# Filler products of a recurrent-attention and feed-forward kernel move to another PSUM bank, with a new order and engine table

## The chip, the cores and the metric

One core of one Trainium2 chip runs the whole program. The metric is the device time of one execution in microseconds (us). Times "from the span's start" count from the first instruction of the profiled execution.

## The reference

A delta-rule recurrence over 768 tokens (4 batches, 8 heads, head width 48) makes `y`; its rows, gathered to 3072 tokens of 384 features, go through a feed-forward layer with 2048 hidden features.

```python
for t in range(S):
    kt, vt, bt = (k_n[:, :, t], v[:, :, t], beta[:, :, t, None])
    y[:, :, t] = np.einsum('bhd,bhde->bhe', q[:, :, t], state)
    v_old = np.einsum('bhde,bhd->bhe', state, kt)
    state = state + bt[:, :, :, None] * np.einsum('bhd,bhe->bhde', kt, vt - v_old)
...
h = x @ w_in
sp = np.maximum(h, 0.0) + np.log1p(np.exp(-np.abs(h)))
g = h * erf(sp)
return (g @ w_out).astype(np.float32)
```

## The kernel before

**Attention.** The 768 tokens are cut into 12 chunks of 64. For each chunk TensorE forms Gram products (`gram_mm`), and DVE scales them (`gram_a`, `gram_p`). They go through DRAM into blocks (`to_dram`, `to_blocks`), and a triangular system of 32x32 blocks is solved row by row for two chunks at a time: `solve_row` (lines 341 to 353), 31 rows, two elementwise operations a row, on DVE for the first pair of chunks and on GpSimd (POOL) for the other five. Each row needs the one before it. The solution comes back (`put_blocks`, `from_blocks2`, or `back_t` and `back_x` for chunks 0 and 1) and is merged (`merge_*`). Then the recurrence runs over chunk and batch, 48 steps: `chain_u`, `chain_s` and `chain_y` on TensorE, with DVE and ScalarE (ACT) steps between (`chain_u2`, `chain_s2`, `chain_y2`, `chain_m`).

**Feed-forward.** Four steps of the recurrence make a group of 256 tokens; there are 12 groups. The input is split into a high and a low fp16 part (`x_hi`, `x_lo`), and so are the two weights, once, at the start (`w_load`, `w_mask`, `w_sign`, `w_bits`, `w_mx`, `w_hi`, `w_lo`). A group has 16 blocks of 128 hidden features. `ffn1` (line 683) is the first stage: nine products for one block. Two blocks share one PSUM bank and make a *unit*, 8 units to a group. On each unit ACT computes softplus (`e_sp`, line 715) and erf (`e_erf`, line 720), DVE multiplies the bank by the result (`e_mul`, line 724), and `e_split` and `e_rest` make the fp16 parts. `ffn2` (line 736) is the second stage: six products per block into two of three banks `pr`. Softplus and erf lie in different function tables of ACT, so `table` (line 161) loads a table (`ACT_TABLE_LOAD`, line 164) whenever the wanted one is not there.

**Banks.** PSUM has 8 banks: three for the attention (`psa`), two for the first stage (`ps1`, tag `ph`), three for the second (`pr[0]` to `pr[2]`). A buffer of a pool is given to a new tile when every use of the old tile is past. Group g's `ffn2` uses `pr[2g % 3]` and `pr[(2g + 1) % 3]`: group 0 uses `pr[0]` and `pr[1]`, group 1 `pr[2]` and `pr[0]`. At the start `pr` also serves Gram products, the splitting of `w_in` (`w_lo1`), and the first four recurrence steps.

**Filler products.** `warm` (line 174) multiplies a zero tile by itself into a bank that it takes once from `ps1`; nothing reads it. It runs 15 times at the start, and 264 events `fill` (line 181) issue one such product each at chosen places of TensorE's queue.

```python
    def warm(n):
        if not wp:
            wp.append(ps1.tile([P, FW], F32, tag="ph", name="warm"))
        for _ in range(n):
            te.matmul(wp[0], zero[:, :P], zero, start=True, stop=True)
    def fill():
        warm(1)
```

**Order and engines.** Every step is an event, registered by `on`. `ORDER` (line 34) is a permutation of the 2505 events, written out by hand, and the events are issued in it; each engine, and SyncE's queue (SP) of DMA issues, works through its own instructions in that order. `ENG` (line 35) names an engine for 17 events in place of the step's own choice (`pick`, line 112). Before the first `ffn1` TensorE's queue holds 15 + 182 filler products; behind it stand 82, the last two just ahead of the spread of group 2's maximum (`x_all` of group 2).

Of the kernel before, what the change touches and what calls it, by code (L numbers as in the profile page):

```python
# [15 lines left out]
P = 128  # L16
# [18 lines left out]
ENG = {374: "G", 488: "V", 758: "A", 766: "A", 783: "V", 790: "A", 820: "A", 937: "V", 1051: "V", 1158: "V", 1319: "V", 1461: "V", 1465: "G", 1469: "G", 1663: "A", 2005: "V", 2175: "V"}  # L35
LEAD = 3
MD = 4.4
CS = 1.2
WARM = 15
C2 = 12.0  # L40
C3 = 16.0
SS2 = 12.8
S1 = -2.5
SPL = 32
XT = (0, 1)
UM = 32
DZ = 64
WG = -6
WU = 264
MT = 58  # L50
M1 = 0
WL = (0.9, 0.95, 1.0, 1.05, 1.1, 1.15, 24, 24.1, 31.0, 32.5, 34.0, 35.5)
WK = (6.0, 6.7, 7.4, 8.1, 8.8, 9.5, 28, 29, 36.0, 37.5, 39.0, 40.5)
WF = (6.6, 7.3, 8.0, 8.7, 9.4, 10.1, 28.6, 29.6, 36.6, 38.1, 39.6, 41.1)
WI = (17.0, 18.0, 19.0, 20.0, 21.0, 22.0, 31, 32, 50.5, 52.1, 53.7, 55.3)
WOT = (36, 38, 40, 42, 76, 78, 62, 86, 88, 90, 72, 74)
WD = 0.4
LPE = ("in",)
RI = "HLHLHLHLHLHH"
RO = "LHLHLHLHLHHH"  # L60
LMI = [0] * 16
# [24 lines left out]
def delta_ffn_kernel(ctx, tc, kT, qT, ktok, vtok, btok, w_in, w_out, cst, out):  # L86
    nc = tc.nc
    te, ve, se, ge, sp = nc.tensor, nc.vector, nc.scalar, nc.gpsimd, nc.sync
# [10 lines left out]
    pr = [ps2.tile([P, 512], F32, name=f"pr{i}") for i in range(PB)]  # L99
# [7 lines left out]
    def on(t, fn, *a, **kw):  # L107
        ev.append((t, len(ev), lambda: fn(*a, **kw)))
# [3 lines left out]
    def pick(d):  # L112

        return ENG.get(cur[0], d)

# [17 lines left out]
    def us(x):  # L133
        return (x - T0) / SW
# [22 lines left out]
    zero = ff.tile([P, FW], F16, tag="ob", bufs=2, name="zero")  # L157
# [13 lines left out]

    wp = []
# [7 lines that stand above are left out]

    def fill():
        warm(1)

    def clear_q():
        for t in qp[0] + qp[1]:
            ge.memset(t, 0.0)

    def clear_x():
        for t in xm[0] + xm[1]:
            se.copy(t.rearrange("p (a x) c -> p a (x c)", a=4), zero[:, :256].unsqueeze(1).broadcast_to([P, 4, 256]))  # L190
        for t in zz:
            se.copy(t.rearrange("p a h d -> p a (h d)"), zero[:, :2 * DZ].unsqueeze(1).broadcast_to([P, NP, 2 * DZ]))

    def load_cst():
        sp.dma_start(mask, cst[:, P:])
        sp.dma_start(ident, cst[:, :P])
# [582 lines left out]
    def gram(t, d, c, name):  # L779

        on(t - 1.5 * d, load_kf, c, "kpg")
        on(t - 1.45 * d, load_kf, c, "qpg")
        for i in range(2):
            on(t + 0.9 * i * d, gram_mm, c, i, name)
            on(t + (0.35 + 0.9 * i) * d, gram_a, c, i)
            on(t + (0.45 + 0.9 * i) * d, gram_p, c, i)
        on(t + 2 * d, put_p, c)

    def norm_events(sg, t, d):
        for x in range(2):  # L790
# [3 lines left out]
            on(t + (0.2 + 0.2 * x) * d, norm_sum, c)  # L794
            gram(t + (0.75 + 1.8 * x) * d, d, c, "pg")
            on(t + (2.05 + 1.8 * x) * d, to_dram, c)
        on(t - 2.3 * d, load_beta, sg)
        for i in range(6):
            on(t + (0.45 + 0.1 * i) * d, norm_ops, sg, i)

    on(-100, clear_first)
    on(-99, clear_second)
    on(-98, warm, WARM)
    for i in range(WU):
        on(us(6 + 0.17 * i), fill)
    on(us(0), clear_q)
    for i, (fn, *a) in enumerate(((load_step, 0), (load_step, 1), (load_beta, 0), (load_kf, 0, "kpg"), (load_kf, 1, "kpg"),
                                  (load_cst,))):
        on(us(0.1 + 0.05 * i), fn, *a)
    on(us(6.5), clear_x)  # L810
    on(us(19), load_q, 0)
    on(us(21), load_q, 1)
    on(us(30), w_ident)
    for sg in range(2):
        t = (4, 20)[sg]
        if sg:
            for i, (fn, a) in enumerate(((load_step, 2), (load_step, 3), (load_beta, 1))):
                on(us(14 + 0.05 * i), fn, a)
# [167 lines left out]

    ev = [ev[i] for i in ORDER] if ORDER else sorted(ev, key=lambda e: e[:2])
    E = mybir.EngineType
# [47 lines left out]
```

## Time and profile before

| | |
|---|---|
| median of 3 runs | 614.65 us (612.47 to 615.39) |
| the profiled execution's own time | 614.14 us |
| its span | 612.4 us |
| busy: TensorE, ScalarE, VectorE, GpSimd | 97%, 85%, 66%, 50% of the span |
| ACT table loads | 165, 211.7 us in all |
| filler products | 279, 392 ns each as the profile draws them |

A busy share is time in which an engine had an instruction in work. Matmuls are pipelined, so the start of one to the start of the next is a better price than the duration drawn. A row ending in `<-` names what ended the engine's idle time before that instruction.

### The profile page before, as it was taken

The page shows a single profiled execution, that of the slowest core. Times are in us where ns is not written, and L with a number is a line of the kernel's source. Part 1 is how long each engine was busy: PE and PEld are TensorE (multiplying, and loading weights), DVE is VectorE, ACT ScalarE, POOL GpSimd, SP SyncE. Part 2 cuts the span into 40 slices and gives each one's busy share as a digit, 9 for nine tenths or more (in the row PEclk, how much of TensorE's full clock was granted, in tenths as well). Part 3 has the DMA queues.
Part 4 walks back from the last instruction along what each step waited for, and adds up shares of the span by engine and source line. Part 5 has one row for each costly group of instructions (what it writes and reads, how often), then busy time and mean ns, then how long its engine had stood idle before and what let it go on. Part 6 is the DMA issues. An engine that isn't in the chain of part 4 may idle for free.

```text
span 612.4 us, 25280 instructions
## 1 busy us (share of the span) xinstructions
PE 591.3 (97%) x11043; PEld 423.4 (69%) x11043; DVE 406.8 (66%) x926; ACT 518.2 (85%) x747; POOL 304.7 (50%) x484
## 2 busy tenths in 40 slices
PE   9999889999999989979999999999999999999996
PEld 3654566666676767767777777777777777777773
DVE  3689996688768878985875986668565665336231
ACT  8979979998886688669878999789979988879873
POOL 3010224898279834987467874289863132203221
PEclk9999999999999999999999999999999999999999
DMA  8999826374554367832583224553045100100021
GB/s 279 338 291 253 220 51 172 117 160 126 111 111 114 94 158 157 195 85 84 129 181 99 76 69 114 108 120 98 1 104 132 48 15 22 28 1 14 2 52 27
DMA packets 86383, 69.74 MB, mean 114 GB/s; under 512 B 64064, under 2 KB 73408, under 8 KB 86272
## 3 DMA queue, kind: packets, MB, share of 16 engines
q1 hardware_dynamic: 86272, 68.12, 43.3%
q8 instruction: 87, 1.43, 1.0%
q14 instruction: 24, 0.20, 0.1%
HBM read 48.17 MB, written 18.87 MB: 109 GB/s over the span
## 4 chain that ended last, share of the span: by engine, by line
PE 70%; DMA 9%; DVE 9%; ACT 5%; issue 3%; POOL 2%; SPq 1%; POOLq 0%; ACTq 0%; DVEq 0%
PE ph L693 27%; PE pr L745 10%; PE pr L747 9%; PE pr L746 9%; PE pc L481 2%; DMA qp<-pp 2%; PE pc L507 2%; DMA raw_in<-w_in 2%; PE warm L179 2%; PE pg L287 2%; PE pm L444 2%; PE pc L511 1%; PE pc L495 1%; DMA raw_out<-w_out 1%; DMA k<-ktok 1%
## 5 line engine op out<-in xcount | busy, mean ns | idle before, releaser
L164 ACT ACT_TABLE_LOAD x165 | 211.7, 1283 | 2.9
L693 PE MATMUL ph<-xh,w_in 128*128 128x256 f16 x1152 | 204.7, 273 | 1.9 <-DVE L L724 1.5
L693 PEld LDWEIGHTS <-w_in 128*128 128x128 f16 x1728 | 166.4, 98 | 31.8 <-issue 3.3
L693 PE MATMUL ph<-xl,w_in 128*128 128x256 f16 x576 | 157.0, 273 | 0.3 <-issue 0.3
L117 POOL TENSOR_TENSOR H<-L,H 128x512 f16<-128x512 f32 x58 | 69.2, 1201 | 145.8 <-DVE H L124 80.8
L745 PE MATMUL pr<-w_out,H 128*128 128x384 f16 x384 | 125.6, 327 | 0.0
L747 PE MATMUL pr<-w_out,H 128*128 128x384 f16 x384 | 125.2, 326 | 0.3 <-issue 0.3
L746 PE MATMUL pr<-w_out,H 128*128 128x384 f16 x384 | 125.2, 326 | 0.0
L724 DVE SCALAR_TENSOR_TENSOR L<-ph,L 128x512 f32<-128x512 f32 x96 | 65.8, 688 | 83.8 <-ACT L L720 70.3
L353 POOL TENSOR_TENSOR xb<-xb,tmptmpg 128x31 f32<-128x31 f32 (+15 forms) x154 | 89.2, 579 | 12.1
L351 POOL TENSOR_TENSOR tmptmpg<-gb,xb 128x31 f32<-128x31 f32 (+15 forms) x154 | 83.2, 540 | 22.0 <-DMA v<-vtok 6.9
L715 ACT ACTIVATE L<-ph,xct 128x512 f32<-128x512 f32 x96 | 65.6, 687 | 28.3 <-PE ph L693 26.3
L117 POOL TENSOR_TENSOR z<-v,nm 64x192 f32<-64x192 f32 x94 | 51.6, 549 | 65.7 <-DMA v<-vtok 50.4
L179 PE MATMUL warm<-zero 128*128 128x512 f16 x279 | 72.6, 392 | 1.2 <-DVE zero L170 1.2
L720 ACT ACTIVATE L<-L 128x512 f32<-128x512 f32 x96 | 59.6, 629 | 0.9
L747 PEld LDWEIGHTS <-H 128*128 128x128 f16 x384 | 37.6, 98 | 25.5 <-issue 0.7
L745 PEld LDWEIGHTS <-H 128*128 128x128 f16 x384 | 37.5, 98 | 22.2
L746 PEld LDWEIGHTS <-H 128*128 128x128 f16 x384 | 37.6, 98 | 19.9
L179 PEld LDWEIGHTS <-zero 128*128 128x128 f16 x279 | 26.1, 100 | 30.1 <-issue 6.2
L487 DVE TENSOR_TENSOR z<-pc,ga 64x192 f32<-64x192 f32 x88 | 31.3, 355 | 17.6 <-PE pc L481 13.0
L122 ACT CAST H<-L 128x512 f16<-128x512 f32 x56 | 33.7, 610 | 9.4 <-DVE L L724 9.3
L500 DVE TENSOR_TENSOR z<-pc,z 48x192 f32<-48x192 f32 x80 | 28.3, 353 | 17.1 <-PE pc L495 13.7
(157 smaller groups left out, 823.8 us busy)
## 6 DMA issues: line engine op xcount, KB each, us to landing
raw_in<-w_in SPq DMA_DIRECT2D x12, 512.0 KB, 9.2
raw_out<-w_out SPq DMA_DIRECT2D x12, 512.0 KB, 7.6
d<-A SPq DMA_DIRECT2D x22, 256.0 KB, 3.5
d<-pp SPq DMA_DIRECT2D x10, 512.0 KB, 4.5
qp<-d SPq DMA_DIRECT2D x20, 256.0 KB, 4.2
kpg<-kT SPq DMA_DIRECT2D x24, 192.0 KB, 4.7
k<-ktok SPq DMA_DIRECT2D x12, 384.0 KB, 5.6
qp<-qT SPq DMA_DIRECT2D x24, 192.0 KB, 3.7
```

The source lines that it names most:

```text
L117: {"V": ve, "G": ge}[pick(d)].tensor_tensor(*a, **kw)
L164: se.add_instruction(mybir.InstLoadActFuncSet(name=nc.get_next_instruction_name(), act_func_set_id=i, ins=[], outs=[]))
L179: te.matmul(wp[0], zero[:, :P], zero, start=True, stop=True)
L351: eng.tensor_tensor(tv, G[:, s, s + 1:].unsqueeze(1).broadcast_to([P, ncol, nr]), Xv[:, :, s:s + 1].broadcast_to([P, ncol, nr]), op=ALU.mult)
L353: eng.tensor_tensor(Xv[:, :, s + 1:], Xv[:, :, s + 1:], tv, op=ALU.add)
L693: te.matmul(ph, w[:, i, kt * P:kt * P + P], G[x][:, :, ksl], start=(m == 0), stop=(m == 8))
L715: se.activation(unit(g, u), G["ph", u], AF.Softplus, bias=0.0, scale=G["ct"])
L720: se.activation(Lu, Lu, AF.Erf, bias=0.0, scale=1.0)
L724: ve.scalar_tensor_tensor(Lu, fg[g]["ph", u], HSC, Lu, op0=ALU.mult, op1=ALU.mult)
L745: te.matmul(G["po"][a], gh[:, o, asl], wout_h[:, i, :], start=(i == 0), stop=False)
L746: te.matmul(G["po"][a], gh[:, o, asl], wout_l[:, i, :], start=False, stop=False)
L747: te.matmul(G["po"][a], gl[:, o, asl], wout_h[:, i, :], start=False, stop=(i == NFF - 1))
```

## The change

82 filler products are taken out, all that stood behind the first `ffn1` in TensorE's queue. 50 others, `fill2`, are put in behind it; they write `pr[2]` and not the tile taken from `ps1`. They stand between `chain_s` of step 2 and `merge_e` of chunk 2. The remaining 15 + 182 all stand ahead of the first `ffn1`.

`ORDER` is a new permutation of the now 2473 events. Read by name, TensorE's queue keeps its sequence but for short moves: `ffn1` of unit 6 of group 1 moves ahead of `gram_mm` of chunk 5, and between the `ffn1` of the first two units of group 0, where a Gram product, five filler products and a merge stood, the filler products are gone. On SP, `from_blocks2` of chunk 2 moves ahead of `to_dram` of chunk 4, and the loads of the first two chunks' keys move behind nine `w_load` of `w_in`. On ACT, `clear_x` moves from the first place to behind seven steps on `w_in` and two `norm_sq`.

`ENG` now has 153 entries, and some 140 events take another engine. Between the first `ffn1` and `x_all` of group 2: 13 rows of the second and third solve go from POOL to DVE (6 of solve 1, 7 of solve 2; an eighth of solve 2 follows later, while its row 21 goes back to POOL); 14 events leave ACT (five `e_split` and two `w_hi` to POOL, the other seven to DVE) and 5 come to it; three `e_rest` go from DVE to POOL and two the other way; three `put_v` go to DVE. Ahead of the first `ffn1`: eight `w_sign` and two `w_mx` go from ACT to DVE, five `back_x` the other way, two `w_hi` to POOL, and rows 0 and 24 of the first solve to POOL. In the order of events ACT has 163 table loads, 27 between the first `ffn1` and `x_all` of group 2 where there were 31.

```diff
...
-WU = 264
+WU = 182
+WV = 50
...
+    def fill2():
+        te.matmul(pr[2], zero[:, :P], zero, start=True, stop=True)
+
...
     for i in range(WU):
         on(us(6 + 0.17 * i), fill)
+    for i in range(WV):
+        on(us(6 + 0.17 * (WU + i)), fill2)
...
```

## Rows read from the trace of the kernel before

**Rows 1.** Stretches of the span, busy us (xinstructions): PE, PEld, DVE, ACT, POOL; clock, DMA

```profile
0.00:92.00 92.00, 85.55 (x1436) 48.48 (x1437) 71.15 (x193) 79.36 (x167) 14.66 (x27) 1.00 0.82 238
92.00:134.10 42.10, 40.48 (x753) 26.89 (x751) 29.83 (x62) 39.70 (x54) 30.62 (x51) 1.00 0.61 157
134.10:178.60 44.50, 43.33 (x711) 30.81 (x710) 32.20 (x58) 39.40 (x52) 28.06 (x50) 1.00 0.49 113
178.60:194.60 16.00, 15.80 (x563) 11.59 (x563) 12.26 (x29) 10.51 (x19) 14.36 (x23) 1.00 0.23 60
194.60:230.60 36.00, 33.20 (x928) 25.65 (x927) 28.44 (x74) 28.07 (x41) 22.09 (x40) 1.00 0.57 149
230.60:312.40 81.80, 78.36 (x1682) 60.68 (x1678) 63.01 (x140) 68.44 (x94) 54.07 (x89) 1.00 0.56 132
312.40:426.00 113.60, 113.60 (x2422) 86.39 (x2421) 84.03 (x187) 99.14 (x133) 78.06 (x129) 1.00 0.44 107
```

**Rows 2.** The chain that ended last, 97 to 103 us: start, duration, engine and line

```profile
97.30 0.70 DVE L L724
...
98.05 2.14 PE ph L693 x18
...
100.21 0.69 ACT L L715
...
100.91 1.28 ACT L164
...
102.21 0.64 ACT L L720
...
102.87 0.70 DVE L L724
```

**Rows 3.** Line 724 (`e_mul`) from 91 to 200 us: min/median/max ns, first and last start

```profile
L724 DVE SCALAR_TENSOR_TENSOR L<-ph,L x16: 673/691/694, 97.3 to 198.1; 128x512 f32<-128x512 f32 x16
```

**Rows 4.** The filler products (line 179) alone, 92 to 194.6 us: PE and PEld busy

```profile
92.00:194.60 102.60, 22.66 (x83) 7.27 (x82) 1.00 0.50 123
```

**Rows 5.** TensorE in order of time, 32 to 37 us: 17 filler products and the next

```profile
32.85 3.84 PE L179 MATMUL warm<-zero 128*128 128x512 f16 x17
36.53 0.38 PE L544 MATMUL spin<-ident,m_in 128*128 128x128 f32 x2
```

**Rows 6.** `chain_s` of step 2 on TensorE, `chain_s2` of steps 2 and 1 on DVE

```profile
100.97 0.57 PE L495 MATMUL pr<-z,k 64*48 64x48 f32 x32
...
103.48 1.47 DVE L500 TENSOR_TENSOR z<-pr,z 48x192 f32<-48x192 f32 x4
```

**Rows 7.** Row 21 of solve 2, the one solved on DVE, between rows on POOL

```profile
202.11 0.61 POOL L351 TENSOR_TENSOR tmptmpg<-gb,xb 128x231 f32<-128x231 f32 x1
202.80 0.63 POOL L353 TENSOR_TENSOR xb<-xb,tmptmpg 128x231 f32<-128x231 f32 x1
...
203.46 0.39 DVE L351 TENSOR_TENSOR tmptmpg<-gb,xb 128x220 f32<-128x220 f32 x1 [1.99 <-POOL xb L353]
...
204.42 0.57 POOL L351 TENSOR_TENSOR tmptmpg<-gb,xb 128x207 f32<-128x207 f32 x1 [0.99 <-DVE xb L353]
```

**Rows 8.** A small DVE operation and two operations of POOL at the same time

```profile
150.94 2.61 DVE L253 SCALAR_TENSOR_TENSOR gn<-t,ri 128x32 f32<-128x32 f32 x1
...
151.24 2.26 POOL L117 TENSOR_TENSOR H<-L,H 128x512 f16<-128x512 f32 x2
```

**Rows 9.** SP's issues around `from_blocks2` of chunk 2 (line 393)

```profile
155.34 1.08 SPq L324 DMA_DIRECT2D d<-A  x2
156.52 3.31 SPq L393 DMA_DIRECT2D xm<-d  x4
```

**Rows 10.** ACT at the start: the second half of `clear_x`, the first step on `w_in`

```profile
5.82 3.21 ACT L192 CAST z<-zero 128x512 f32<-128x512 f16 x6
...
12.29 0.67 ACT L568 ACTIVATE raw_in<-raw_in 128x512 int32<-128x512 uint16 x1 [1.78 <-DMA raw_in<-w_in]
```

More of the change, by code (lines that the diff above doesn't have):

```diff
@@ new lines @@
+ENG = {312: "G", 336: "G", 342: "G", 351: "A", 359: "A", 360: "A", 361: "A", 362: "A", 369: "V", 372: "V", 373: "V", 379: "V", 381: "V", 382: "V", 435: "V", 436: "V", 439: "V", 440: "V", 441: "V", 442: "V", 443: "V", 456: "V", 457: "V", 582: "V", 583: "V", 662: "V", 670: "V", 689: "V", 693: "V", 702: "A", 705: "A", 710: "A", 721: "A", 726: "A", 734: "A", 740: "A", 742: "A", 743: "V", 750: "A", 751: "A", 753: "A", 758: "A", 759: "V", 785: "A", 786: "V", 788: "A", 799: "V", 801: "A", 804: "A", 806: "A", 807: "V", 818: "V", 863: "V", 880: "V", 905: "A", 925: "V", 934: "V", 939: "V", 942: "V", 1019: "G", 1024: "V", 1041: "V", 1050: "V", 1084: "V", 1104: "V", 1126: "V", 1129: "V", 1152: "V", 1163: "V", 1180: "V", 1203: "V", 1260: "V", 1265: "V", 1267: "V", 1270: "V", 1285: "V", 1287: "V", 1290: "V", 1300: "V", 1302: "V", 1305: "V", 1310: "V", 1403: "G", 1406: "G", 1429: "A", 1433: "G", 1435: "G", 1437: "G", 1439: "G", 1463: "G", 1508: "G", 1509: "G", 1513: "G", 1518: "V", 1519: "G", 1534: "V", 1544: "V", 1545: "V", 1553: "V", 1555: "V", 1592: "G", 1593: "G", 1597: "G", 1607: "G", 1618: "V", 1627: "G", 1631: "V", 1677: "G", 1681: "G", 1687: "G", 1691: "G", 1697: "G", 1701: "A", 1702: "V", 1707: "G", 1715: "A", 1721: "V", 1723: "V", 1765: "A", 1766: "V", 1780: "V", 1786: "V", 1796: "V", 1799: "A", 1844: "G", 1849: "G", 1859: "G", 1864: "V", 1865: "G", 1869: "A", 1875: "G", 1879: "A", 1938: "G", 1949: "G", 1953: "G", 1973: "V", 2012: "V", 2023: "G", 2028: "V", 2037: "A", 2038: "V", 2097: "G", 2117: "G", 2121: "A", 2143: "V", 2190: "G", 2196: "V", 2200: "G", 2219: "A", 2269: "A", 2349: "G", 2468: "V", 2471: "A"}
```

3 lines of the change are left out of this document (1 added, 2 removed).

## The prediction

> **What bounds the kernel now.** I read the busy time by stretches first. From 312 us on TensorE is busy all the time, and from 194.6 to 312 nearly so [rows 1]: there the end is set by TensorE's own work, and whatever starts that work earlier ends the kernel earlier. The clock is granted in full (2.4 GHz) in every one of these stretches. What can be won therefore lies ahead of 194.6 us, and in the 2.8 + 3.4 us that TensorE idles between 194.6 and 312.4 [rows 1].
>
> Between 92 and 194.6 us TensorE looks busy too, but 83 of its products there are fillers [rows 4]. One costs (36.53 - 32.85) / 17 = 0.216 us in a run of them [rows 5], so the 82 behind the first `ffn1` are 17.7 us of 102.6 with nothing in them. Why they are needed the chain of waits shows. It goes round a loop: `e_mul` of a unit (0.70), then `ffn1` of the next (2.14), softplus (0.69), a table load (1.28), erf (0.64), `e_mul` [rows 2]. `ffn1` starts 0.05 us after `e_mul` has ended. That is what a single first-stage bank looks like, and the code has one: `warm` holds the other from the start until its last use, and a buffer passes on only when all uses are past, so the 82 late fillers hold it until 194.6 us. One turn takes 102.87 - 97.30 = 5.57 us; the 16 units in this stretch come at (198.1 - 97.3) / 15 = 6.7 us [rows 3].
>
> **The change, part by part.** The sum is made against the profiled execution's 614.14 us, 0.5 below the median of the runs.
>
> *The bank.* The last filler to the first-stage tile now stands ahead of the first `ffn1`, so both banks turn. `ffn1` of the next unit can run while ACT works on this one, and the loop loses its 2.14 us of TensorE. What a unit then needs at least is ACT's share: two table loads, softplus and erf, 2 x 1.28 + 0.69 + 0.64 = 3.9 us [rows 2], below the 6.7 us at which units come. Here a rule can be held against the row. In the loop the erf starts 0.02 us after its table load has ended [rows 2], so a load costs 1.28 us and no more. The Trainium skill (ScalarE: Activation LUTs, section What ACT_TABLE_LOAD costs) gives about 2.66 us for each change of table, a drain included; by that a unit would need 6.6 us on ACT and the second bank would give nothing. By the rows it gives room.
>
> *TensorE's sum, 92 to 194.6 us.* The work stays but for its order; I take it as unchanged. 32 fillers fewer: 32 x 0.216 = 6.9 us. Its idle time there is 1.6 + 1.2 + 0.2 = 3.0 us [rows 1], all of which could go. Against that stands a new wait. The first `fill2` writes `pr[2]`, which `chain_s2` of step 2 on DVE still reads. In the kernel before `chain_s` ends at 101.54 and the two steps of `chain_s2` at 104.95, of which step 2 takes the first half, to 104.2 [rows 6]: 2.7 us if DVE comes to it as late as now, 0.7 us if it comes at once. Queued behind on TensorE is `merge_m` of chunk 1, and for that ACT and DVE wait. I take 2.7, the row as it stands, and 1.0 us more for one later wait of the size that a handoff between POOL and DVE shows [rows 7]. Sum: -6.9 - 3.0 + 3.7 = **-6.2 us**; at best -9.9, at worst 0, if another engine takes the place of the bank.
>
> *Can the others follow?* ACT is busy 39.7 + 39.4 + 10.5 = 89.6 of 102.6 us [rows 1]. Nine steps net leave it, 0.6 to 0.7 us each by operations of the same size [rows 2], and four table loads of 1.28: about 11 us less, 79 in 96: not the bound. DVE has 29.8 + 32.2 + 12.3 = 74.3 us [rows 1]. It takes 13 rows of the solves at 0.78 us (two operations of 0.39 [rows 7]), 10.1 us, and about 2 us net of smaller steps: 86 in 96. DVE is late next. POOL gives the rows away and takes five `e_split`; its 73.0 us [rows 1] hardly change.
>
> *The solves.* On POOL a row takes 203.43 - 202.11 = 1.32 us; the row on DVE, both handoffs included, 204.42 - 203.43 = 0.99 [rows 7]. 0.33 us a row makes 2.0 us for the 6 rows of solve 1 and 2.3 for solve 2, net of row 21 that goes back. `from_blocks2` of chunk 2 now stands ahead of `to_dram` of chunk 4, whose issue it followed directly [rows 9]; the two issues of `to_dram` are 1.1 us, and the wait for `gram_a` of chunk 4 goes with them. So the attention can follow an earlier feed-forward, and I book only solve 2, against TensorE's 6.2 us of idle time up to 312.4: **-2.3 us** (0 to -6.2). `to_dram` of chunk 4 comes later by the 3.3 us of the four issues that now precede it [rows 9], inside the several us won on solve 1.
>
> *Ahead of the first `ffn1`.* ACT is busy 79.4 of 92 us [rows 1] and loses eight `w_sign` and two `w_mx`, some 7 us. But `clear_x`, which now ends at 9.03 us, ahead of the first tile of `w_in` at 12.29 [rows 10], moves to behind seven steps on `w_in`: its cover is gone, and it costs what it takes, over twice the 3.2 us of its second half. DVE has 71.2 of 92 us and takes the ten steps. The two nearly cancel: 0, from -4 (ACT's gain counts alone) to +3 (the second half of `clear_x` counts alone). The keys loaded later delay the Gram products; `fill` covers that on TensorE, and DVE's `gram_a` has `w_sign` to do before it. Price: in the +3.
>
> *Moves of engine behind 312 us* have one answer: TensorE has no idle time there, so 0 while every engine keeps ahead.
>
> Sum: 614.14 - 6.2 - 2.3 + 0 = 605.6; set against the median, **606 us**.
>
> **Rivals.** *DVE takes the bank's place.* DVE then works 86 us of the stretch. Now it idles 28 us there. If 15 of those remain, since its steps wait for TensorE and ACT in turn, the stretch takes 101.3 us, 1.3 less than now, and with nothing won later the kernel takes 613. For it: `e_mul`, which frees the bank, stands on DVE behind solve rows. Against it: part of DVE's idle time is now the wait for erf.
>
> One more thing makes DVE later. The small step `gn` took 2.61 us, over just the time that POOL had two operations of 2.26 us running [rows 8]. The Trainium skill (SBUF — State Buffer, section Who interferes with whom) says that a DVE instruction with two SBUF inputs contends with a GpSimd instruction that reads SBUF, and the second to issue blocks until the first is done. By that each `e_split` on POOL may hold a solve row on DVE for its whole length; the trace agrees, but it does not show how often they meet.
>
> *Slower: the handoffs.* A solve row on DVE waits for POOL's row before it, and DVE can do nothing else meanwhile: 1.99 us in the one case [rows 7]. If each of the 13 rows waited so, DVE would need 86 + 26 = 112 us, the stretch would take 10 us more than now, and the kernel 624. It decides from where 13 waits exceed what DVE has left, 96 - 86 = 10 us: 0.8 us a row. Against it: rows that follow one another on DVE (6 and 7, 15 and 16, 4 to 8 of solve 2) wait once.
>
> *The start gains as well.* If ACT's relief counts in full, 4 us and some of TensorE's other idle time come on top: 600.
>
> *Nothing happens.* If the bank were not released at the last first-stage filler, the loop would stay at 5.57 us a unit, the fillers would only have been cover, and the time would be 614. The code speaks against it. The same time would come if a table load held ACT for twice what its row shows, since a unit would then need as much on ACT as the loop takes now; the erf that starts 0.02 us behind its load speaks against that [rows 2], and I give it 0.01. The figure of the Trainium skill above, taken for both loads, would lead there.
>
> **How the numbers follow.** Forecast 0.60, start gains too 0.15, DVE takes over 0.12, handoffs 0.08, nothing 0.04, long table loads 0.01. About 0.5% (3.1 us) is what a measurement of this kernel can tell from no change. Faster: 0.60 + 0.15 + 0.05 of DVE's case = 0.80; same: the other 0.07, 0.04 and 0.01 = 0.12; slower 0.08. The range reaches from the second case with some of the -9.9 bound, 598, to DVE's case, 613.
>
> **What would show it.** Right: `ffn1` of a unit no longer starts at the end of the unit's `e_mul` before it; the units of the first two groups come at under 6.4 us; 50 fillers between 92 and 190 us; `x_all` of group 2 some 6 us earlier; the first `fill2` waits for `chain_s2` on DVE. Wrong: the first `ffn1` far from 92 us; DVE busy over 95% of the stretch with `e_mul` late after erf; `e_mul` waiting on solve rows of POOL; or idle time of TensorE behind 312 us.

## The result, and the profile after

The changed kernel takes **621.09 us** (median of 4 runs, 618.95 to 624.35), against 614.25 of the kernel before beside it: a ratio of 1.0119, 95% interval 1.0074 to 1.0163. Run again, it gave 1.0153 [1.0079, 1.0227]. It is slower by over 1%, where 606 was forecast. The profiled execution took 620.85 us with a span of 619.1, 6.7 longer than before.

The stretches of the changed kernel, with the columns of [rows 1]:

```profile
0.00:92.00 92.00, 84.56 (x1365) 47.85 (x1366) 70.60 (x183) 71.00 (x150) 18.64 (x32) 0.98 0.82 240
92.00:134.10 42.10, 36.09 (x785) 25.96 (x783) 30.61 (x77) 32.48 (x45) 26.00 (x37) 0.96 0.56 135
134.10:178.60 44.50, 44.50 (x732) 32.14 (x734) 38.03 (x82) 40.00 (x55) 29.69 (x47) 1.00 0.57 127
178.60:194.60 16.00, 15.26 (x559) 11.19 (x549) 14.29 (x34) 8.97 (x18) 13.06 (x20) 1.00 0.41 92
194.60:230.60 36.00, 32.28 (x847) 25.04 (x842) 28.38 (x71) 27.66 (x39) 22.03 (x38) 0.95 0.46 120
230.60:312.40 81.80, 80.08 (x1774) 61.20 (x1766) 62.04 (x138) 69.58 (x96) 54.62 (x94) 1.00 0.62 150
312.40:426.00 113.60, 111.06 (x2367) 83.93 (x2366) 77.58 (x181) 97.83 (x129) 72.85 (x120) 1.00 0.40 97
```

Two things are new. TensorE idles where it did not, 6.0 us between 92 and 134.1 (1.6 before) and 2.5 behind 312.4 (none before). And the clock is no longer granted in full in three of the stretches.

What the change was to do, it did. Between the first `ffn1` (95.0 us now, 92.0 before) and `x_all` of group 2 (195.8, 194.6 before) there are 50 fillers instead of 82. Line 186 alone in that stretch, as in [rows 4]:

```profile
95.00:195.80 100.80, 12.97 (x50) 4.92 (x50) 0.98 0.53 123
```

`e_mul`, now line 728, comes as in [rows 3], a unit in (199.3 - 100.6) / 15 = 6.6 us:

```profile
L728 DVE SCALAR_TENSOR_TENSOR L<-ph,L x16: 670/678/692, 100.6 to 199.3; 128x512 f32<-128x512 f32 x16
```

No wait of TensorE ahead of `ffn1` is put down to `e_mul` there any more (4 before, 1.5 us). The first `fill2` waits for `chain_s2`, as [rows 6] had it, 1.98 us where 2.7 were booked:

```profile
104.23 1.46 PE L186 MATMUL pr<-zero 128*128 128x512 f16 x6 [1.98 <-DVE z L504]
```

**Where the time went.** The largest new idle time stands in the middle of a row of 16 small products that have all they need. TensorE in order of time, the changed kernel, then the kernel before where its largest pause of this kind between 92 and 194 us stands:

```profile
113.51 0.29 PE L511 MATMUL pc<-qp,z 128*32 128x64 f32 x6
117.42 0.53 PE L511 MATMUL pc<-qp,z 128*32 128x64 f32 x9 [3.62 <-issue]
```
```profile
111.57 0.27 PE L693 MATMUL ph<-xh,w_in 128*128 128x256 f16 x1
112.12 0.28 PE L693 MATMUL ph<-xh,w_in 128*128 128x256 f16 x1 [0.29 <-issue]
```

"issue" says that TensorE waited for nothing that the profile shows. If TensorE's instructions (weight loads, products and the few of its sequencer) are numbered from 0 in order of time, both pauses stand ahead of number 3777, which is 193 + 14 x 256. From here on a *block* is such a run of 256 instructions. So do the other pauses over 0.3 us, of these two kernels and of the three that are told first below, ahead of an instruction that waits for no semaphore: all at 193 plus a multiple of 256, but for the first instruction of each program. The DMA queue "q8 instruction" moves one 16 KB packet for each 256 instructions of TensorE (86 packets, 22,151 instructions). The packet that was needed at 113.8 us started at 114.5, 4.4 us after TensorE had entered the block ahead of it at 110.06, and took 1.5 us. The DMA queues of the changed kernel in the two stretches (packets, MB, share of 16 engines):

```profile
q1 hardware_dynamic: 389, 0.86, 104.3%
...
q1 hardware_dynamic: 124, 0.43, 90.9%
q8 instruction: 1, 0.02, 5.7%
```

The first line is 110.1 to 114.4 us, the others 114.4 to 116.1: the packet of code starts after 4.4 us in which packets of data fill the engines. That it stands in line behind them is tested below. In the kernel before the block of the same numbers held 10 fillers and lasted 6.2 us; its packet started 3.0 us after the block was entered, and the pause at its end was 0.28 us.

Behind the pause the clock falls to 1.2 GHz. Three stretches (columns as above): the pause, then up to 120.4 us, then up to 123.8:

```profile
113.80:117.40 3.60, 0.00 (x1) 0.00 (x0) 3.42 (x10) 3.55 (x5) 1.43 (x4) 0.94 0.99 305
117.40:120.40 3.00, 2.98 (x61) 1.99 (x62) 1.41 (x4) 2.11 (x5) 2.68 (x5) 0.51 0.95 237
120.40:123.80 3.40, 3.40 (x26) 2.34 (x24) 1.02 (x3) 1.69 (x2) 3.09 (x5) 1.00 0.03 10
```

Added up over the traces (idle time of TensorE in pieces over 0.25 us, the last six instructions left out; half clock ahead of 604 us):

```
                           before   after   difference
idle ahead of 193 + 256k      1.9    12.8     +10.9 us
other idle time of TensorE   12.4     8.9      -3.5
half clock, 10.2 us / 2         0     5.1      +5.1
32 fillers x 0.216                             -6.9
sum                                            +5.6   (span: +6.7)
```

The half-clock line takes it that TensorE has full work there and does half of it, which makes it a bound from above. So at least 1.1 us of the 6.7 are not accounted for.

### The profile page after: what moved, and what is told of

It is laid out like the page before. It is cut to its first block, busy times and chain, and to the rows that moved or that the text cites. A ratio compares the mean times of both kernels' runs of the same rounds, so it can differ in the third digit from the quotient of the medians.

```text
span 619.1 us, 25197 instructions
## 1 busy us (share of the span) xinstructions
PE 590.7 (95%) x11011; PEld 424.1 (69%) x11011; DVE 412.6 (67%) x964; ACT 505.2 (82%) x725; POOL 302.7 (49%) x463
## 4 chain that ended last, share of the span: by engine, by line
PE 84%; DMA 5%; DVE 3%; ACT 3%; issue 3%; POOL 1%; SPq 0%; POOLq 0%; ACTq 0%
PE ph L697 30%; PE pr L749 11%; PE pr L751 10%; PE pr L750 10%; PE pc L485 3%; PE pc L511 2%; DMA raw_in<-w_in 2%; PE pg L291 2%; PE warm L180 2%; PE pm L448 2%; PE pr L186 2%; PE pc L499 2%; PE pc L515 2%; DMA v<-vtok 1%; PE pe L416 1%
## 5 line engine op out<-in xcount | busy, mean ns | idle before, releaser
L165 ACT ACT_TABLE_LOAD x163 | 209.1, 1283 | 3.6 <-PEq L1035 0.7
L118 POOL TENSOR_TENSOR H<-L,H 128x512 f16<-128x512 f32 x61 | 71.2, 1178 | 126.5 <-DVE H L125 55.8
L355 POOL TENSOR_TENSOR tmptmpg<-gb,xb 128x135 f32<-128x135 f32 (+15 forms) x136 | 75.3, 554 | 34.4 <-DVE xb L357 15.6
L357 POOL TENSOR_TENSOR xb<-xb,tmptmpg 128x135 f32<-128x135 f32 (+15 forms) x136 | 78.2, 575 | 10.7
L118 POOL TENSOR_TENSOR z<-v,nm 64x192 f32<-64x192 f32 x82 | 47.9, 585 | 67.5 <-DMA v<-vtok 47.6
L180 PE MATMUL warm<-zero 128*128 128x512 f16 x197 | 48.7, 393 | 1.5 <-DVE zero L171 1.2
L504 DVE TENSOR_TENSOR z<-pc,z 48x192 f32<-48x192 f32 x80 | 28.3, 354 | 15.5 <-PE pc L499 11.3
L180 PEld LDWEIGHTS <-zero 128*128 128x128 f16 x197 | 18.9, 101 | 25.2 <-issue 5.9
L123 ACT CAST H<-L 128x512 f16<-128x512 f32 x49 | 29.5, 610 | 8.0 <-DVE L L728 7.9
```

The lines of the kernel that those rows point to most:

```text
L118: {"V": ve, "G": ge}[pick(d)].tensor_tensor(*a, **kw)
L165: se.add_instruction(mybir.InstLoadActFuncSet(name=nc.get_next_instruction_name(), act_func_set_id=i, ins=[], outs=[]))
L355: eng.tensor_tensor(tv, G[:, s, s + 1:].unsqueeze(1).broadcast_to([P, ncol, nr]), Xv[:, :, s:s + 1].broadcast_to([P, ncol, nr]), op=ALU.mult)
L357: eng.tensor_tensor(Xv[:, :, s + 1:], Xv[:, :, s + 1:], tv, op=ALU.add)
```

## The experiments

Theory A: TensorE waits for its own code at every 256th instruction when the DMA engines are full, and the clock falls behind such a wait; fillers gave the code its time, and the places of the blocks decide the rest. Against it stood B (semaphores or the new order), C (the engine table) and later D (what the test kernels do to the start). In the table "stalls" is the idle time (pieces over 0.25 us) ahead of instructions 193 + 256k in the run's trace, and the clock the mean over its timed runs. A ratio compares with runs of before made beside it; medians of different lines compare less well, since before itself moved between 614.25 and 615.76. The trace is one execution: that of h_pro_sh64 took 614.1 us and that of b_thin 619.6, both well above their medians.

> The kernel after the change once more, unaltered, beside the others of this group, since its first comparison rests on 4 runs. 618 to 622 by the median, granted clock 0.985 to 0.99.

| run | median us | ratio to before, 95% | clock | stalls us |
|---|---|---|---|---|
| before | 614.25 to 615.76 | 1 | 0.995 | 1.9 |
| after | 621.09 | 1.0119 [1.0074, 1.0163] | 0.987 | 12.8 |
| after2 (after again) | 620.87 | 1.0153 [1.0079, 1.0227] | 0.983 | 11.3 |
| a_sh32 | 618.24 | 1.0025 [0.9997, 1.0054] | 0.991 | 6.8 |
| a_sh64 | 617.11 | 1.0019 [0.9991, 1.0048] | 0.990 | 6.9 |
| b_sh32 | 619.26 | 1.0047 [1.0026, 1.0069] | 0.991 | 7.3 |
| b_bank | 613.89 | 0.9972 [0.9951, 0.9993] | 0.995 | 2.7 |
| b_bank_sh64 | 618.82 | 1.0039 [1.0010, 1.0068] | 0.991 | 4.3 |
| b_thin | 615.79 | 1.0006 [0.9979, 1.0033] | 0.991 | 4.1 |
| a_thin | 618.11 | 1.0025 [0.9999, 1.0052] | 0.985 | 12.6 |
| b_bank_thin | 614.24 | 0.9999 [0.9960, 1.0038] | 0.986 | 2.0 |
| a_engB | 639.60 | 1.0391 [1.0361, 1.0422] | 0.983 | 10.9 |
| a_move | 620.51 | 1.0105 [1.0059, 1.0150] | 0.991 | 9.3 |
| h_pro | 619.01 | 1.0048 [1.0017, 1.0080] | 0.990 | 12.4 |
| h_pro_sh32 | 618.06 | 1.0053 [1.0026, 1.0080] | 0.988 | 13.6 |
| h_pro_sh64 | 610.08 | 0.9943 [0.9912, 0.9973] | 0.993 | 7.0 |
| h_pro_sh96 | 611.73 | 0.9945 [0.9913, 0.9977] | 0.993 | 6.4 |
| h_pro_sh128 | 618.48 | 1.0042 [1.0018, 1.0066] | 0.989 | 11.3 |
| h_pro_dma | 617.89 | 1.0012 [0.9973, 1.0050] | 0.991 | 10.8 |
| h_pro_sh96_dma | 612.03 | 0.9961 [0.9929, 0.9994] | 0.992 | 6.2 |

### Moving the code by part of a block

a_sh32 and a_sh64 (from after) and b_sh32 (from before) split the first 32 or 64 filler products, far ahead of everything else, in two halves: the same columns, 64 or 128 instructions more.

```diff
+SH = 32
...
     def fill():
+        if 2 < cur[0] < 3 + SH:
+            for h in range(2):
+                te.matmul(wp[0][:, :256], zero[:, :P], zero[:, :256], start=True, stop=True)
+            return
         warm(1)
```

> The kernel after the change, with its first 32 filler events issuing two products of 256 columns in place of one of 512: the same columns and the same TensorE time, but 64 TensorE instructions more (a weight load and a product each), so that everything later in TensorE's program stands 64 places further on. The trace of the changed kernel has stalls of TensorE that stand at every 256th of its instructions, 193 on from a multiple of it (3.61 us at 113.8, 2.43 at 199.6, 1.35 at 336.6, 1.19 at 382.3), just where a 16 KB packet of the queue named instruction is late. Theory A (TensorE waits for its own code, behind the data on the DMA engines): the places of the stalls move 64 instructions back in the order of events, their sizes change, and the time changes by 1 us or more, in either direction; the block that ended at 113.8 then ends ahead of chain_y.4. The fall of the clock to half behind a stall goes where the stall goes. Theory B (semaphores or the new order make these stalls): they stay at the same products (chain_y of step 4, chain_u of step 14) with the same sizes, and the time is that of the changed kernel within 1 us (621).

> As the run with 32 split fillers, but with 64 of them (128 TensorE instructions, half a block of 256). Theory A: the stalls stand another 64 instructions earlier in the order of events, with other sizes; time between 614 and 626. Theory B: same places, same sizes, 621 within 1 us.

> The kernel before the change with the same 64 instructions more ahead of its first products. Theory A: its code blocks then begin at other products; where a block comes to lie on a stretch with no fillers while the DMA engines are full, a stall of 1 to 4 us appears that the kernel before does not have; time 612 to 622. Theory B: 614 within 1 us, no new stall.

Measured: the 3.6 us at `chain_y` of step 4 is gone in both versions of after, and the pauses stand at 193 + 256k as before, now ahead of other products: with 64, ahead of an `ffn1` (2.67 us at 119.4). In a_sh32 the instructions behind 312 us have nearly the numbers again that they have in before, and its pauses there come to 0.5 us, in after to 3.2. The kernel before gets what it did not have, pauses of 1.3 us at 74.6, 1.1 at 113.3, 1.6 at 199.9 and 2.2 at 204.6 us, and half clock ahead of 604 us, 10.2 us in all. It loses 0.47% by nothing but 64 instructions more; after wins some 0.9%. B falls: no semaphore and no order changed.

### The bank alone, and the bank with its code moved

b_bank keeps the order and the engines of before. The 68 fillers between `chain_s2` of step 2 and `ffn2` of tile 16 (a tile is one block of 128 hidden features, counted through the groups) write `pr[2]`, and the 12 ahead of them and the last 2 are left out. b_bank_sh64 has the split of 64 besides.

```diff
+F2 = 197
...
     def fill():
+        if cur[0] >= F2:
+            te.matmul(pr[2], zero[:, :P], zero, start=True, stop=True)
+            return
         warm(1)
```

> The order and the engines of the kernel before, with the move of the bank alone: 68 filler products between chain_s2 of step 2 and ffn2 of tile 16 write a second-stage bank, the 12 fillers ahead of chain_s2 of step 2 and the last 2 are left out. The prediction's own step: 14 products less (3.0 us) and the two first-stage banks of the 3.0 us of idle time, less a wait: 609 to 612. Theory A (the fillers give the code fetch its time): 12 of the 14 stood in the blocks of code around 97 to 102 us; what they cost is given back as a stall there, or the blocks behind are 28 instructions displaced: 612 to 618. If the bank alone were the cause of the loss: 618 or more.

> The order and engines of the kernel before with the move of the bank alone (613.9, few stalls), its later code moved by half a block. Theory A: the places were good and a move can as well be a loss, 612 to 620, with stalls of over 1 us at block ends where there were none. Rival D: faster by some us, 606 to 610.

Measured: 613.89, a gain of 0.28% [0.07, 0.49]. No `ffn1` waits for `e_mul` any more, and from the first `ffn1` to `x_all` of group 2 it takes 99.7 us in place of 102.6. The bank is thus not the loss, but its gain is 1.7 us by the ratio and 2.9 in that stretch of the trace, where 14 fillers (3.0 us) and the idle time (3.0 us) were to be won, less a wait. With the code moved by half a block the gain turns into a loss of 0.39% [0.10, 0.68]. The stalls grow by only 1.6 us. TensorE's other idle time grows by 1.3, and half clock ahead of 604 us from 3.4 to 10.2 us, which is worth up to 3.4: together 6.3 of the 6.8 us by which the span grows.

### What a filler costs: thin fillers

b_thin gives the 82 late fillers of before 64 columns in place of 512, a_thin the 50 of after, b_bank_thin the 68 of b_bank. Instructions and places stay. The edit of b_thin:

```diff
+LATE = 185
...
     def fill():
+        if cur[0] >= LATE:
+            te.matmul(wp[0][:, :64], zero[:, :P], zero[:, :64], start=True, stop=True)
+            return
         warm(1)
```

> The kernel before the change with its 82 late fillers at 64 columns in place of 512: the same instructions at the same places of TensorE's code, the same hold on the first-stage bank, but about 0.15 us less of TensorE each, 12 us in all. The prediction's step (a filler is pure cost, since TensorE sets the pace there): 602 to 605. Theory A (a filler buys the time in which the code and the data arrive, and keeps the clock up): most is given back as stalls behind blocks of code, as waits and as stretches at half clock; 609 to 618, with a granted clock below 0.995.

> The kernel after the change with its 50 second-stage fillers at 64 columns in place of 512: same instructions, about 0.15 us less each, 7.5 us in all. A filler as pure cost: 613 to 614. Theory A: 617 to 623, with longer stalls at the same block ends and at least as many stretches at half clock.

> The kernel before with the bank's move alone, and the 68 moved fillers at 64 columns. With thin fillers the kernel before waited for the first-stage bank instead (1 to 2 us at each of seven pairs of ffn1 between 97 and 152 us) and kept its time; here that bank is free. If the bank is the wait that stood behind the fillers' time: 606 to 611, faster than either kernel. If fillers give back what they take through code and clock alone, bank or not: 612 to 616.

Measured: b_thin takes the time of before to 0.06% [-0.21, 0.33]. TensorE in the same stretch, before (92 to 194.6) and b_thin (92 to 195.9), with the columns of [rows 1]:

```profile
92.00:194.60 102.60, 99.60 (x2021) 69.28 (x2020) 74.29 (x148) 89.61 (x123) 73.03 (x122) 1.00 0.50 123
```
```profile
92.00:195.90 103.90, 87.73 (x2022) 66.43 (x2020) 73.26 (x148) 89.68 (x124) 73.74 (x123) 0.98 0.50 122
```

11.9 us less of TensorE's work, and the stretch is not shorter (in an execution of 619.6 us, where the median is 615.8). What ended its waits ahead of `ffn1`, in b_thin:

```profile
  DVE L L728: 10.6, 10
  issue: 0.5, 1
  DVE xl L685: 0.2, 1
```

Waits for `e_mul` are 10.6 us where they were 1.5: the loop of [rows 2] sets the pace, and the fillers had only filled its time. But the bank alone does not set it either: b_bank_thin has no such wait and still takes the time of before, at a clock of 0.986. Its longest waits are now 3.07 us of `chain_y` for DVE (`chain_u2`) at 117.1 and 2.39 for a Gram bank at 148.8. a_thin gains against after by the ratios (1.0025 against 1.0119 and 1.0153), at a clock as low as that of after. The longer stalls that theory A expected there did not come (12.6 us against 12.8 and 11.3).

### The engine table and the start

a_engB is after's order with before's table `ENG`. h_pro is before's order and engines ahead of the first `ffn1`, after's behind it.

```diff
-ORDER = (after ahead of ffn1(0)) + (after behind)
+ORDER = (before ahead of ffn1(0)) + (after behind)
```

> The kernel after the change, its order kept, with the engine table of the kernel before (141 events back on their old engines). TensorE's program is unchanged, instruction for instruction. Theory A: the stalls at 113.8 and 199.6 us stay, and the time with them; 619 to 623. Theory C (the engine table is the loss, through rows of the solve and chain_y2 on VectorE, or back_x and w_mx on ScalarE in the start): 614 to 617, with the first ffn1 back at 92 to 93 us. Worse than 624 if the order of after was made for its table.

> The kernel after the change, but with the order and the engines of the kernel before for everything ahead of the first ffn1 (182 fillers there in both, so that TensorE's instructions behind it keep their places in the blocks of 256). In the traces the first ffn1 starts at 92.0 us before and 95.0 us after. Theory A (three causes add up: a start 3.0 us later, stalls for code, clock): the 3.0 us of the start come back, 617 to 619, and the stall near 114 us stays, as its block holds the same instructions. If the start is hidden by what comes later: 620 to 622. If the start and its engines are the whole loss: 614 to 615.

Measured: with the old table the new order takes 639.6. C falls; the new table is not the loss, and the order was made for it. With the old start it takes 619.0 (ratio 1.0048), 2 us below after by the medians and 4 to 6 by the ratios, and its first `ffn1` is at 91.3 us. The stall is where it was, as its block holds the same instructions:

```profile
109.93 0.29 PE L511 MATMUL pc<-qp,z 128*32 128x64 f32 x7
114.03 0.53 PE L511 MATMUL pc<-qp,z 128*32 128x64 f32 x9 [3.80 <-issue]
```

### Fillers moved into the block that stalls

a_move takes the ten fillers ahead of `ffn1` of tile 20 into the block that ends at the 3.6 us; from tile 20 on all places stay. TensorE's order by name:

```diff
-... ffn1(7) chain_u(7) ... ffn1(15) fill2 x10 ffn1(20) ...
+... ffn1(7) fill2 x10 chain_u(7) ... ffn1(15) ffn1(20) ...
```

> The kernel after the change with ten of its fillers moved: the ten ahead of ffn1 of tile 20 stand ahead of chain_u of step 7, in the dense block of code that ends at the 3.6 us stall at 113.8 us. From ffn1 of tile 20 on every instruction keeps its place in the blocks of 256. Theory A (the stall is the block's lack of length: packet late by 4.4 us, 1.5 us long, 1.4 us until TensorE runs, against 3.7 us of work): ten fillers lengthen the block's work by 2.2 us, so the stall shrinks to 1 to 2 us, the half-clock stretch behind it goes or gets rarer, and as the ten are missing later the time falls by 1 to 4 us against the unaltered kernel after. Theory B (stall made by a semaphore or by the order): it stays at 3 to 4 us and the time within 1 us.

Measured: the stall falls to 0.92 us, as theory A has it. The time does not fall with it clear of the noise (620.5 against 620.9, four runs each): where the ten had stood, `ffn1` now waits for its input, 2 x 1.48 us. The two rows:

```profile
118.37 0.25 PE L515 MATMUL pc<-qp,z 128*32 128x64 f32 x2 [0.92 <-issue]
...
142.41 0.28 PE L697 MATMUL ph<-xh,w_in 128*128 128x256 f16 x1 [1.48 <-DVE xh L132]
144.17 0.27 PE L697 MATMUL ph<-xl,w_in 128*128 128x256 f16 x1 [1.48 <-DVE xl L685]
```

So these ten, too, stood in a gap and cost nothing there. Theory A was right on the stall and wrong on the time.

### Start and place together

h_pro_sh32, 64, 96 and 128 are h_pro with so many fillers of the start split as above. 128 make one whole block.

```diff
+SH = 128
...
```

> Both repairs at once: the start of the kernel before in front of the rest of the kernel after, and 64 of the start's fillers split in two, so that the blocks of code end elsewhere. If the parts add up (start 2 to 4 us, places of the blocks 3 to 4 us, from 621): 613 to 616, level with the kernel before. If the two repairs are of the same time: 617 to 619.

> As the run with 64 split fillers that gave 610, with 32: a quarter of a block from either neighbour. Theory A: no stall at chain_y of step 4; a time set by where the dense blocks meet full DMA engines, between 609 and 618, and not a mean of its neighbours. Rival D: half of the gain, 614 to 615.

> With 96 split fillers, three quarters of a block. Theory A: between 609 and 618, and no stall at chain_y of step 4. Rival D: more gain than with 64, under 610.

> The start of the kernel before, the rest of the kernel after, and 128 split fillers: 256 TensorE instructions more, exactly one block, so that all later code stands at the same places within blocks as with no split filler at all. Theory A (the place of the code in its blocks is what the split of 64 fillers changed, 619 to 610): back to 617 to 620, and the stall of 3 to 4 us ahead of chain_y of step 4 is there again, one block later in the count. Rival D (the split itself, two short products for a long one in the start, is what made it faster): 608 to 611, no such stall.

Measured: 610.1 with 64 and 611.7 with 96, faster than the kernel before by 0.57% [0.27, 0.88] and 0.55% [0.23, 0.87]; 618.1 with 32; and with 128, one whole block, back to 618.5 with the stall back at the same product:

```profile
113.03 0.29 PE L516 MATMUL pc<-qp,z 128*32 128x64 f32 x7
115.76 0.53 PE L516 MATMUL pc<-qp,z 128*32 128x64 f32 x9 [2.43 <-issue]
```

D falls: the most split fillers give nothing, half as many give 8 us by the medians and 6 by the ratios (0.9943 against 1.0042). Neither 610.1, below the sum of the two repairs (613 to 616), nor 618.1, just above the range of theory A (609 to 618), was forecast: theory A tells that the place matters, not which place is good. In h_pro_sh64 the same `chain_y` of step 4 runs through; its stall of the stretch stands ahead of an `ffn1`:

```profile
114.06 0.41 PE L516 MATMUL pc<-qp,z 128*32 128x64 f32 x16
...
119.59 0.28 PE L702 MATMUL ph<-xl,w_in 128*128 128x256 f16 x1 [2.83 <-issue]
```

Within this family the stalls go with the times: 12.4, 13.6 and 11.3 us in the runs of 618 to 619, 7.0 and 6.4 in those of 610 and 612. Across the table they do not: a_sh32 has 6.8 us at 618.2, b_bank_sh64 4.3 at 618.8. The sum of the stalls is one part of the loss; the half clock and the waits for other engines are others.

### Why the packet is late

h_pro_dma issues two loads of q (steps 5 and 7, 768 KB) on SP behind the load of k for step 4 instead of ahead of it. TensorE's program is that of h_pro. h_pro_sh96_dma does the same in h_pro_sh96. SP's order by name:

```diff
-load_v(9) load_kf(5 qpg) load_kf(7 qpg) put_p(3) load_step(5) load_v(13) from_blocks(2) load_kf(4 kpg)
+load_v(9) put_p(3) load_step(5) load_v(13) from_blocks(2) load_kf(4 kpg) load_kf(5 qpg) load_kf(7 qpg)
```

> The start of the kernel before with the rest of the kernel after (619.0), where two loads of q (steps 5 and 7, 768 KB) are issued behind the load of k for step 4 instead of ahead of the stall near 110 us. TensorE's program is the same to the instruction. Theory A with its second half (the packet of code is late because it stands behind data on the DMA engines): the block that is entered at 106.5 us and got its packet 4.7 us later gets it 1.5 to 3 us later, so the stall of 3.8 us ahead of the rest of chain_y of step 4 falls to 0.5 to 2.5 us; the time falls by 1 to 4 us, unless the two loads hold up the next packets. If the packet's time has nothing to do with the loads: stall 3.5 to 4 us, time within 1 us of 619.

> The same two loads moved in the version with 96 split fillers (611.7), as a try at the best version. Its stalls stand at 113.2 (1.9 us), 181.0 (1.4) and 199.1 us (2.0); the first falls if theory A holds, 609 to 612; the other two have other loads in front. Loads that come late for step 5: 612 to 616.

Measured: the packet comes 2.2 us after the block is entered and not 4.7, and the stall of 3.80 us becomes

```profile
113.74 0.29 PE L511 MATMUL pc<-qp,z 128*32 128x64 f32 x7
114.82 0.35 PE L511 MATMUL pc<-qp,z 128*32 128x64 f32 x9 [0.79 <-issue]
```

The code waits behind data. In the time 617.9 against 619.0 (1.0012 against 1.0048) is inside the intervals: a new stall at 191.9 us (1.5 us) takes part of it back. In the other version the stall near 113 us falls from 1.9 to 1.0, and the time does not change (612.0 against 611.7).

## Why the prediction was wrong

The parts of the sum beside the two traces, from the first `ffn1` (91.95 us before, 94.96 after) and the rows of `x_all` of groups 2 and 5, before and after:

```profile
194.64 0.38 PE L544 MATMUL sp<-ident,xm 128*128 128x128 f32 x2
312.35 0.38 PE L544 MATMUL sp<-ident,xm 128*128 128x128 f32 x2
...
195.78 0.39 PE L548 MATMUL sp<-ident,xm 128*128 128x128 f32 x2
313.45 0.39 PE L548 MATMUL sp<-ident,xm 128*128 128x128 f32 x2
```

| part, us | booked | measured |
|---|---|---|
| up to the first `ffn1` | 0 | +3.0 |
| to `x_all` of group 2 | -6.2 | -1.9 |
| to `x_all` of group 5 | -2.3 | 0.0 |
| to the last product | 0 | +5.3 |
| behind it | not named | +0.3 |
| sum | -8.5 | +6.7 |

The step that failed is that a filler taken out and an idle time closed were booked as time won, in a sum with no term for TensorE waiting for its own code and none for a lower clock. The trace of after shows 10.9 us more of pauses for code and up to 5.1 us of half clock; the largest single miss is the 0 behind 312 us.

**"What can be won lies ahead of 194.6 us, 82 fillers with nothing in them."** Here it failed first. The term -6.9 for 32 fillers came as worked out: TensorE's busy time from the first `ffn1` to `x_all` of group 2 fell by 5.2 us, from 99.6 to 94.4, and half clock at 116.9 us can hide up to 1.7 more. But a filler was priced at what it takes and not at what stands ready to take its place; that the fillers were cover was named for the rival "nothing happens" alone. In b_thin 11.9 us less of them shorten nothing. Some covered the waits of the loop, some the way of the code, and they kept the clock up: fillers of 64 columns lower the mean clock in b_thin and b_bank_thin by 0.004 and 0.009.

**"Its idle time there is 3.0 us, all of which could go", less 3.7 of waits.** It became 100.8 - 94.4 = 6.4 us: 1.98 for `chain_s2` (2.7 booked, right in kind), and 3.6 of the stall. The kernel before has such pauses too, five of 0.28 to 0.70 us; they were read as nothing. The wait for `chain_s2` had a second price that was not booked. In seven of the fourteen traces of the new order half clock starts within 1.4 us of the end of this wait (1.9 to 2.6 us there), with no pause for code over 0.3 us in the 5 us ahead. In after2 the same six fillers that took 1.46 us above take 2.72:

```profile
103.19 2.72 PE L186 MATMUL pr<-zero 128*128 128x512 f16 x6 [1.94 <-DVE z L504]
```

So not all of the lost clock stands behind code; some of it comes with the move of the bank itself. The stretch gained 1.9 us for the 6.2 forecast.

**"The clock is granted in full in every stretch."** True of the profiled execution of before (0.999), and taken as given for after. Over 132 timed runs of the kernel before the clock is 0.995 in the mean, and the time goes with it, 0.46 us for each 0.001 (47 runs at 0.997 and more: 614.0 us; 34 at 0.993 and less: 617.0). At that rate the 0.987 and 0.983 of after go with 4 and 6 us of the 6 to 9 lost. How much of that is the clock itself and how much the stalls ahead of its falls, the slope does not tell.

**"Ahead of the first `ffn1`: 0, from -4 to +3."** 3.0 us later in the first profile, 1.4 in the second: inside the bounds, toward their bad end. By h_pro the start as a whole costs 2 us by the medians and 4 to 6 by the ratios. In the other places of the code it costs nothing (a_sh32 and h_pro_sh32, ratios 1.0025 and 1.0053) or 5 us (a_sh64 and h_pro_sh64, 1.0019 and 0.9943). Which of its steps cost what was not tried.

**"The solves: -2.3."** From `x_all` of group 2 to that of group 5 it took as long as before, 117.7 us. Two stalls of code (2.43 us at 199.6, 0.65 at 232.9) and half clock behind the first are in that. In h_pro_sh96 the same way takes 114.6 us, 3.1 less, and in h_pro_sh32 120.1. So the step can be right, eaten by the stalls and the clock; that the solves are what gains there is not shown.

**"Moves behind 312 us have one answer: 0."** From there to the last product it took 5.3 us more. One `ffn2` (1.0 us) had moved to behind that point; stalls of 1.35, 1.19 and 0.63 us at 336.6, 382.3 and 466.7 make 3.2; about 1 us is not accounted for. The other runs part the two causes. From `x_all` of group 5 to the last product it takes 294.8 to 295.7 us in the six traces of the old order; in the new order 299.5 to 302.1 in the eight whose later code lies in its blocks as in after, and 296.1 to 296.8 in the six where it lies elsewhere. The new order itself thus costs 1 to 2 us there, and its place in the blocks 3 to 5. The reason given, that TensorE has no idle time there, speaks of gains alone: 64 instructions fewer put the ends of the later blocks at other products, and a stretch with no idle time can be given some.

**The rivals.** None was this one. Table loads stayed at 1.28 us (163 of them, 209.1 us). The slower rival, handoffs of the solve rows, had the right sign by the wrong way: DVE is busy 80.8 of the 100.8 us and is not the bound. Of the signs of a wrong forecast that were named, two came: the first `ffn1` far from 92 us, and idle time of TensorE behind 312 us. Of the signs of a right one two failed: the units came at 6.6 us and not under 6.4, and `x_all` of group 2 later and not 6 us earlier.

**What stays.** The change, its start put back and its code half a block further on (h_pro_sh64), takes 610.1 us and beats both kernels; h_pro_sh96 does it in the same measure. That is 0.55% and not the 1.4% forecast, and it is the better half of four places tried; the other two are slower than before by 0.5%. The kernel before was tried at two places, 0.47% apart. So what the bank and the new order are worth at equal luck with the place is not shown. The place alone was worth 1% within the h_pro family, more than the whole gain.

## What to carry to other kernels

Ask of every filler, and of any work taken off TensorE, what would then be waited for: give it an eighth of its columns first and see whether the time falls. When a program of small products changes by some instructions, compare the idle time put down to "issue" before and after, since a result within 1% may come from where the blocks of 256 instructions end. Try the kernel at two or three places of its code before a small change is called a loss or a gain, and look which loads are queued where the products are smallest: moving two of them cut the pause here, though not the time clear of the noise.

## What the runs showed of the hardware that was not expected

TensorE's code comes in 16 KB blocks of 256 instructions by DMA, one block ahead: the changed kernel has 86 packets for 22,151 instructions. In the twenty traces 112 pauses of over 0.5 us stand at block ends. 111 of them end 1.2 to 1.7 us after the packet of the next block has landed, one 1.0 us after. If the packets are counted to the blocks in order, one each, the packet starts 0.65 us after the first instruction of a block where less than half of the DMA engines' time in the first 1.5 us is taken (median of 907 blocks), and 1.9 us after it where over 95% is taken (363 blocks), up to 6.2 in a block that stalled (h_pro_sh96_dma). In 428 of the 1730 blocks it starts ahead of that first instruction, by up to 3.1 us; what asks for it does not show in the traces. A block of the smallest products is used up in 2.1 us, so that even an early packet leaves 1.35 us of idle time (336.6 us in the changed kernel: the packet started 0.8 us after the block was entered, with the DMA engines at 10% until then).

The Trainium skill (Runtime: NRT & Kernel Launch, section Instruction fetch mechanics) describes this fetch in blocks of 256 instructions by the sequencer's own DMA queue, and calls the cost of a block's end mostly hidden. The traces agree on the block and the queue. They do not agree on the cost: 12.8 us in the changed kernel, up to 3.8 at one block's end.
